# Attention, a dense expert layer and soft mixture on one core: the score exponentials one step later, values and scores in fixed PSUM banks

## The chip, the cores and the metric

The kernel runs on one core of one Trainium2 chip. The metric is the device time of one execution in microseconds (us). Engines go by the profile's names: PE does the matmuls (PEld is its weight load), DVE is VectorE, ACT is ScalarE, POOL is GpSimd, SP issues the DMAs. Each engine executes its own instructions in the order in which the kernel wrote them.

## What is computed

Windowed attention with eight memory keys (4 batches, 8 heads, 768 positions, chunks of 32 queries against 56 keys and the 8 memory keys), a dense layer with a SiLU, and a soft mixture of 8 experts with 4 slots each. Cut to what matters:

```python
# attention, per chunk of 32 queries
scores = scale * np.matmul(q_c, k_full.transpose(0, 1, 3, 2))
scores = scores - np.max(scores, axis=-1, keepdims=True)
a = np.exp(scores)
a = a / (np.sum(a, axis=-1, keepdims=True) + 1e-09)
out[:, :, c_start:c_end] = np.matmul(a, v_full)

# dense layer on x = attention output, 3072 tokens x 512
h = x @ w_in                               # 512 -> 2048
g = h * (1.0 / (1.0 + np.exp(-h)))
x = g @ w_out                              # 2048 -> 512

# soft mixture: logits = x @ phi, 32 slots
d = exp(logits - logits.max(0)); d /= d.sum(0)      # dispatch
slot_input = d.T @ x                                # 32 x 512
slot_out[e] = np.maximum(slot_input[e] @ w1[e], 0) @ w2[e]
c = exp(logits - logits.max(1)); c /= c.sum(1)      # combination
return c @ slot_out
```

## The kernel before

**Tiling.** The 3072 tokens are cut into seven blocks (`BLOCKS`, 256, 384, four of 512, and 384 tokens), numbered j = 0 to 6. The attention works on 24 groups g of 128 tokens. A block's dense layer is done in 16 steps i, one for each slice f of 128 hidden units. Blocks 0 and 1 and the attention that feeds them are written out by hand in a table of words (`OPENING`). From about 120 us on, the loop over j = 2 to 6 and i = 0 to 15 is used, and all that follows is about this loop.

**One step of the loop.** In the order of the code: `emit_h` puts 12 matmuls of 512 columns into one of two PSUM banks that alternate (0 and 1; name `ps_h`, line L399); then the first list of the step, `run(j, i, 0)`; then `g_tanh` (ACT, L419, reads `ps_h`), `g_mult` (DVE, L423, reads the same bank and frees it), `g_turn` (DVE transpose, L427); then the second list, `run(j, i, 1)`. Since `ps_h` has two banks, the matmuls of step i + 2 can't start before `g_mult` of step i is done. I write tanh(i), mult(i) and h(i) for the tanh, the multiply and the 12 matmuls of step i.

**What the lists hold.** Two helpers fill them.

`place(j, i, values, scores)` lays out a piece of the attention of the next block, at steps 5, 8, 11 and 14 (in block 2 also at step 1, there without values). In the first list of step i stand the matmuls of the values of one group (`a_values_turned`, name `ps_x`, L352) and of the scores of the group two further on (`a_scores`, name `ps_s`, L266). In the second list of step i stand the copies of the values (`a_hi` on ACT, L186, and `a_lo` on DVE, L382), the row maxima of the scores (`a_max`, DVE, L274, with L278 where a group lies at a sequence's edge), the subtraction of them (`a_sub`, DVE, L287, with a memset L290 at an edge) and the exponential (`a_exp`, ACT, L293, in place). In the second list of step i + 1 stand the sum (`a_sum`, DVE, L297), the reciprocal (`a_inv`, L300 and L301) and the scaling on POOL (`a_norm`, L191).

`routing(j, i, b)` lays out the soft mixture's work on block b: at steps i + 3 and i + 4 the slot sums (`route_slots`, PE, name `ps_a`, L544, in banks 4 to 7) and their addition into `acc` (`route_acc`, DVE, L555, four instructions, one for each bank in the order 4 to 7; all four in one step for block 1), at i + 7 `route_c` (the combination weights' maximum and subtraction on DVE, L563 and L564, and their exponential on ACT, L565), at i + 9 their normalization (`route_cn`, DVE, L571 to L574). i is 0, and 4 for block 1, whose routing runs in block 2 together with that of block 0.

At steps 2, 6, 9, 12 and 15 (from step 15 of block 2 to the end of block 5) the second list also has a conversion of a weight tile (`wo_conv`): two ACT instructions (L206, L208), then one on DVE (L214) that needs both. `v_turn` (DVE, L339 and L343) transposes a group's weights, one step before its values are computed or a little earlier.

**Banks.** A tile asked for with bank `None` gets the next of a ring of four (4, 5, 6, 7 in this loop), by `mbank`. Scores take two from the ring, then values two, and so on. Counted out, every pair of scores in this loop gets banks 5 and 6, and every pair of values 7 and 4.

**The end.** In the last block the loads of the experts' weights start (`load_ew`), each into a buffer as it comes free; behind the loop follow the experts and the combination, on PE, with 64 tiles of 512 KB to load.

Of the kernel before, what the change touches and what calls it, by code (L numbers as in the profile page):

```python
# [17 lines left out]
BLOCKS = [256, 384, 512, 512, 512, 512, 384]  # L18
# [34 lines left out]
def attn_moe_softmoe_kernel(  # L53
# [15 lines left out]
    L = NB - 1  # L69
    win, woutt, wout = (w.bitcast(U32).rearrange("f p (n two) -> f p n two", two=2) for w in (win64, woutt64, wout64))  # L70
    tok0 = [sum(BLOCKS[:j]) for j in range(NB)]
# [42 lines left out]
    call = const.tile([128, NT, 32], F32, name="call")  # L114
# [6 lines left out]
    def bank(b, shape, name):  # L121
        if b is None:
            return mbank(shape, name)
        return psum.tile(shape, F32, tag=f"b{b}", name=name)

    def mbank(shape, name):
        misc[1] += 1
        return bank(misc[0][misc[1] % len(misc[0])], shape, name)
# [125 lines left out]
    xh_t, xl_t, ps_t, a_t, mx_t, sm_t, at_t = {}, {}, {}, {}, {}, {}, {}  # L254
# [62 lines left out]
    def a_values(g, *bs):  # L317
        if g >= FIRST_TURNED:
            return a_values_turned(g)
        AT, vt = at_t.pop(g), v_t.pop(g)  # L320
        px = ps_t[g] = [bank(b, [128, 2, 128], "ps_x") for b in bs or (None, None)]
        for c in range(4):
            q = slice(32 * c, 32 * c + 32)
            for u in range(2):
                for s, r in ((0, 0), (1, 1), (0, 1), (1, 0)):
                    k, h = slice(64 * s, 64 * s + 64), slice(64 * r, 64 * r + 64)
                    n = 2 * r + u
                    nc.tensor.matmul(px[s][h, u, q], vt[k, n, c], AT[k, n, q], start=True, stop=True)  # L328
# [15 lines left out]

    def a_values_turned(g):
        AT, vt = at_t.pop(g), v_t.pop(g).rearrange("p a b c -> p (a b c)").rearrange("p (h a e) -> p h a e", h=8, a=2)
        px = ps_t[g] = [bank(None, [128, 4, 64], "ps_x") for _ in range(2)]
        for a in range(2):
            for p in range(4):
                for s, r in ((0, 0), (1, 1), (0, 1), (1, 0)):  # L350
                    k, h = slice(64 * s, 64 * s + 64), slice(64 * r, 64 * r + 64)
                    nc.tensor.matmul(  # L352
                        px[s][h, 2 * (p % 2) + p // 2, 32 * a:32 * a + 32], vt[k, 4 * r + p, a], AT[k, 4 * r + p, a],
                        start=True, stop=True,
                    )
# [203 lines left out]
    def route_c(j):  # L559
        nt, d0 = BLOCKS[j] // 128, tok0[j] // 128  # L560
        cs = call[:, d0:d0 + nt]
        mx = sm_p.tile([128, nt, 1], F32, tag="cm", name="cm")
        nc.vector.tensor_reduce(out=mx, in_=cs, axis=AX.X, op=ALU.max)  # L563
        nc.vector.tensor_tensor(out=cs, in0=cs, in1=mx.to_broadcast([128, nt, 32]), op=ALU.subtract)  # L564
        nc.scalar.activation(out=cs, in_=cs, func=ACTF.Exp)  # L565

    def route_cn(j):
        nt, d0 = BLOCKS[j] // 128, tok0[j] // 128
        cs = call[:, d0:d0 + nt]
        cm = sm_p.tile([128, nt, 1], F32, tag="cs", name="cs")  # L570
        nc.vector.tensor_reduce(out=cm, in_=cs, axis=AX.X, op=ALU.add)  # L571
        nc.vector.tensor_scalar(out=cm, in0=cm, scalar1=1e-9, scalar2=None, op0=ALU.add)
        nc.vector.reciprocal(out=cm, in_=cm)
        nc.vector.tensor_tensor(out=cs, in0=cs, in1=cm.to_broadcast([128, nt, 32]), op=ALU.mult)  # L574
# [16 lines left out]
    def load_ew(*places):  # L591
        for p in places:
            if not ew_order:
                ew_free.append(p)
                continue
            m = ew_order.pop(0)
            nc.sync.dma_start(out=p, in_=(w1 if m < 32 else w2)[m % 32])
            ew_t[m] = p
# [4 lines left out]
    def words(t, lo, hi):  # L603
        return [t[:, o:o + 1024] for o in range(lo, hi, 1024)]
# [21 lines left out]
    def at(j, i, half, fn, *args, first=False):  # L626
        work = slots.setdefault((j, i, half), [])
        work.insert(0 if first else len(work), (fn, args))


    def place(j, i, values, scores):
        if values is not None:
            at(j, i, 0, a_values, values)
            at(j, i, 0, load_v, values + 1)
            at(j, i, 1, a_hi, values)
            at(j, i, 1, a_lo, values)
        if scores < NG:
            at(j, i, 0, a_scores, scores)
            at(j, i, 0, load_qk, scores + 1)
            at(j, i, 1, a_max, scores)  # L640
            at(j, i, 1, a_sub, scores)
            at(j, i, 1, a_exp, scores)
            at(j, i + 1, 1, a_sum, scores)
            at(j, i + 1, 1, a_inv, scores)
            at(j, i + 1, 1, a_norm, scores, "p")

    def routing(j, i, b):
        at(j, i, 0, route_keep, b)
        at(j, i + 1, 0, route_sum, b)
        at(j, i + 1, 0, route_max, b)  # L650
        at(j, i + 1, 1, route_exp, b)
        at(j, i + 1, 1, route_turn, b)
        at(j, i + 2, 1, route_call, b)
        at(j, i + 3, 0, route_slots, b)
        at(j, i + 3, 1, route_acc, b, range(4) if b == 1 else (0, 1))
        at(j, i + 4, 1, route_run, b)
        if b != 1:
            at(j, i + 4, 1, route_acc, b, (2, 3))
        at(j, i + 7, 1, route_c, b)
        at(j, i + 9, 1, route_cn, b)  # L660

    QUADS = {2: (8, 11, 14), L: (5, 8, 12)}
    ZLAG = {2: 3}
    for b in (0, 1):
        routing(2, 4 * b, b)
    for j in range(3, NB):
        at(j, 0, 0, logits, j - 1, f_order(j - 1)[-1] // 4)
        routing(j, 0, j - 1)

    TURNS = {2: (0, 4, 7, 10, 13)}  # L670
    for n, i in enumerate((1, 5, 8, 11, 14)):
        g = tok0[3] // 128 - 1 + n
        at(2, TURNS[2][n], 1, v_turn, g + 1)
        place(2, i, g if n else None, g + 2)
    for j in range(3, L):
        for n, i in enumerate((5, 8, 11, 14)[:BLOCKS[j + 1] // 128]):
            g = tok0[j + 1] // 128 + n
            if g + 1 < NG:
                at(j, i - 1 if n else 3, 1, v_turn, g + 1, first=(n == 0))
            place(j, i, g, g + 2)  # L680
# [10 lines left out]
    with tc.manual_schedule():  # L691
# [127 lines left out]
        for c in range(4):  # L819
# [5 lines left out]
            )  # L825
        load_ew(*words(z, 5120, NF * BLOCKS[L]))
        route_c(L)
        route_cn(L)

        def expert1(qd, cs, ph):  # L830
# [203 lines left out]
```

## Time and profile before

| | |
|---|---|
| median of three runs | 488.1 us (486.65 to 488.53) |
| the profiled execution, its own time | 487.32 us |
| its span, first to last instruction | 485.5 us |
| PE busy | 451.4 us, 93% |
| PEld busy | 340.0 us, 70% |
| DVE busy | 344.1 us, 71% |
| ACT busy | 185.0 us, 38% |
| POOL busy | 43.8 us, 9% |
| mean granted TensorE clock | 0.966 of full speed |

The profiled execution took 1.8 us more than its span, and stands 0.8 us below the median. A row of a timeline gives the start, the duration, the engine, the line, the operation, and in brackets how long the engine stood idle before it and which instruction ended that. The span of a matmul is modelled: consecutive matmuls of one h(i) overlap in the rows, so that the time from start to start is what one costs. Rows of the same kind are merged (x2, x36); their duration is then that of the whole group.

### The profile page before, as it was taken

To read this page: it belongs to the slowest core of one execution; us is meant where nothing else is said; L and a number is where in the kernel's file an instruction comes from. 1 tells how busy PE (TensorE), PEld (TensorE's weight loads), DVE (VectorE), ACT (ScalarE), POOL (GpSimd) and SP (SyncE) were. 2 spreads that over 40 slices of the span, in tenths; PEclk is the share of its full clock that TensorE was granted. 3 is DMA by queue.
4 is the path that set the end of the run, shared out by engine and by line. 5 is a ranking of instruction groups with operands and counts; after the bars stand their busy time and mean duration, and the time that the engine had idled before them with its cause. 6 is when DMAs were issued, how large, how long until landed. Compare 5 with 4: busy or idle time off the path is not lost.

```text
span 485.5 us, 14527 instructions
## 1 busy us (share of the span) xinstructions
PE 451.4 (93%) x6373; PEld 340.0 (70%) x6373; DVE 344.1 (71%) x770; ACT 185.0 (38%) x388; POOL 43.8 (9%) x41
## 2 busy tenths in 40 slices
PE   5799999999998989999799999899999999999981
PEld 2689888988785667677667678676787789543641
DVE  4827797887898888888888778888875665531161
ACT  3648787873332123233324133351333222211041
POOL 0412134200000001010011011110100000000000
PEclk9659999999999999999999999999999999999996
DMA  8937687554130224124441234311222997799998
GB/s 329 373 139 269 253 300 284 173 200 141 53 96 13 89 93 176 52 96 140 140 139 63 77 134 168 137 69 45 90 88 96 393 408 275 278 412 408 407 355 267
DMA packets 29728, 93.68 MB, mean 193 GB/s; under 512 B 2784, under 2 KB 9184, under 8 KB 29664
## 3 DMA queue, kind: packets, MB, share of 16 engines
q1 hardware_dynamic: 29664, 92.74, 52.0%
q8 instruction: 50, 0.82, 0.7%
q14 instruction: 14, 0.11, 0.1%
HBM read 86.44 MB, written 6.29 MB: 191 GB/s over the span
## 4 chain that ended last, share of the span: by engine, by line
PE 69%; DVE 18%; DMA 5%; ACT 3%; issue 2%; SPq 1%; DVEq 0%; ACTq 0%
PE ps_h L399 41%; PE ps_a L544 5%; PE ps_l L442 4%; DVE garena L423 3%; PE ps_o L868 3%; DVE z L427 3%; PE ps_e L836 3%; PE ps_x L328 3%; DMA oarena<-in_woutt_dram 2%; DMA oarena<-in_win_dram 2%; PE ps_s L266 2%; PE ps_x L352 2%; DVE oarena L343 1%; PE ps_f L918 1%; ACT garena L419 1%
## 5 line engine op out<-in xcount | busy, mean ns | idle before, releaser
L399 PE MATMUL ps_h<-x,w 128*128 128x512 f32 (+2 forms) x704 | 154.3, 364 | 4.5 <-DVE garena L423 3.9
L399 PE MATMUL ps_h<-x1a,w 128*128 128x512 f32 (+2 forms) x544 | 140.7, 364 | 5.1 <-DVE garena L423 3.9
L399 PEld LDWEIGHTS ps_h<-x,w 128*128 128x128 f32 x704 | 126.3, 192 | 25.8 <-DVE garena L423 5.3
L399 PEld LDWEIGHTS ps_h<-x1a,w 128*128 128x128 f32 x544 | 99.6, 189 | 26.8 <-issue 7.7
L423 DVE SCALAR_TENSOR_TENSOR garena<-garena,ps_h 128x512 f32<-128x512 f32 (+2 forms) x112 | 68.0, 607 | 56.6 <-ACT garena L419 55.7
L419 ACT ACTIVATE garena<-ps_h 128x512 f32<-128x512 f32 (+2 forms) x112 | 59.3, 532 | 121.4 <-PE ps_h L399 109.3
L427 DVE STREAM_TRANSPOSE z<-garena 128x512 f32<-128x512 f32 (+2 forms) x112 | 70.1, 631 | 4.0 <-PE ps_a L544 0.4
L191 POOL TENSOR_TENSOR aarena<-aarena,smm 128x512 f32<-128x512 f32 x19 | 22.7, 1194 | 237.2 <-DVE smm L301 213.9
L214 DVE SCALAR_TENSOR_TENSOR oarena<-oarena 128x512 uint32<-128x512 uint32 x46 | 32.5, 720 | 5.3 <-ACT oarena L208 5.2
L206 ACT ACTIVATE oarena<-oarena 128x512 f32<-128x512 f32 x46 | 30.3, 665 | 14.7 <-DMA oarena<-in_win_dram 10.3
L293 ACT ACTIVATE aarena<-aarena 128x512 f32<-128x512 f32 x20 | 12.6, 632 | 50.0 <-DVE aarena L287 27.6
L208 ACT ACTIVATE oarena<-oarena 128x512 uint32<-128x512 uint16 x48 | 31.7, 668 | 0.0
L544 PE MATMUL ps_a<-z,d 32*32 32x512 f32 x768 | 27.0, 598 | 0.6 <-DVE d L515 0.6
L399 PE MATMUL ps_h<-x1b,w 128*128 128x512 f32 x64 | 25.0, 391 | 0.0
L442 PE MATMUL ps_l<-garena,aarena 128*32 128x512 f32 (+2 forms) x216 | 25.0, 543 | 0.0
L274 DVE TENSOR_REDUCE mx<-ps_s 128x4 f32<-128x256 f32 x48 | 17.8, 411 | 5.9 <-PE ps_s L266 5.9
L191 POOL TENSOR_TENSOR w<-oarena,w 128x512 fp32r<-128x512 f32 x12 | 15.7, 1307 | 55.1 <-ACT w L186 55.1
L544 PEld LDWEIGHTS ps_a<-z,d 32*32 32x32 f32 x768 | 12.1, 103 | 11.7 <-issue 7.0
L266 PE MATMUL ps_s<-aarena 64*32 64x64 f32 x1280 | 17.2, 224 | 0.7 <-DMA aarena<-in_qk_dram 0.7
L555 DVE SCALAR_TENSOR_TENSOR acc<-acc,al,ps_a 128x512 f32<-128x512 f32 x20 | 13.9, 742 | 2.5 <-PE ps_a L544 2.4
L266 PEld LDWEIGHTS ps_s<-aarena 64*32 64x32 f32 x1280 | 13.9, 105 | 2.1 <-DMA aarena<-in_qk_dram 0.8
L287 DVE TENSOR_TENSOR aarena<-ps_s,mx 128x256 f32<-128x256 f32 x40 | 14.8, 410 | 0.1
(202 smaller groups left out, 459.1 us busy)
## 6 DMA issues: line engine op xcount, KB each, us to landing
aarena<-in_qk_dram SPq DMA_DIRECT2D x20, 608.0 KB, 5.4
aarena<-in_v_dram SPq DMA_DIRECT2D x20, 512.0 KB, 4.2
w<-in_w_dram SPq DMA_DIRECT2D x20, 512.0 KB, 7.2
oarena<-in_win_dram SPq DMA_DIRECT2D x16, 512.0 KB, 5.4
oarena<-in_woutt_dram SPq DMA_DIRECT2D x16, 512.0 KB, 5.6
oarena<-in_wout_dram SPq DMA_DIRECT2D x16, 512.0 KB, 3.2
z<-in_w_dram SPq DMA_DIRECT2D x10, 512.0 KB, 7.6
oarena<-in_w_dram SPq DMA_DIRECT2D x9, 512.0 KB, 10.2
```

The source lines that it names most:

```text
L191: (nc.gpsimd if eng == "p" else nc.vector).tensor_tensor(**kw)
L206: nc.scalar.activation(out=x, in_=hi_w.bitcast(F32), func=ACTF.Prelu, scale=REBIAS, alpha=-(2.0**32))
L208: nc.scalar.activation(out=lo_w, in_=raw.bitcast(U16)[:, :, 1], func=ACTF.Copy, scale=2.0**-13, bias=-4095.75 / 8192)
L214: nc.vector.scalar_tensor_tensor(out=xb, in0=xb, scalar=3, in1=lo_w, op0=ALU.logical_shift_left, op1=ALU.bitwise_or)
L266: nc.tensor.matmul(ps[r][q, p], t[h, p, q], t[h, p, w:w + 64], start=True, stop=True)
L274: nc.vector.tensor_reduce(out=mx[:, 4 * r:4 * r + 4], in_=ps_t[g][r], axis=AX.X, op=ALU.max)
L399: nc.tensor.matmul(ph, w_t[f][:, wi, 128 * c:128 * c + 128], x[c], start=(c == 0 and m == 0), stop=(c == 3 and m == 2),)
L419: nc.scalar.activation(out=g_tile(j, f), in_=h_t[j, f], func=ACTF.Tanh, scale=0.5)
L423: nc.vector.scalar_tensor_tensor(out=g, in0=g, scalar=1.0, in1=h_t.pop((j, f)), op0=ALU.add, op1=ALU.mult)
L427: nc.vector.transpose(out=z_view(j)[:, slot], in_=g_t[j, f])
L442: nc.tensor.matmul(rt[j, "pl"][32 * m:32 * m + 32], wp[:, f], g_t[j, f], start=(k == ks[0]), stop=(k == ks[-1] or j == L and m > 1 and k = ...
L544: nc.tensor.matmul(ps[q][32 * cg:32 * cg + 32], d[p, t], zv[p, :, t], start=(b < 4), stop=(b >= nb - 4), tile_position=(32 * q, 32 * cg),)
```

## The change

Three edits, all in the lists of the loop. The table `OPENING` and the arithmetic are as they were.

- `a_exp` goes from the second list of step i into that of step i + 1. It keeps its place ahead of `a_sum`.
- The exponential of `route_c` becomes a function of its own, `route_ce`, and goes from the second list of step 7 into that of step 8 (of steps 7 and 11 into those of steps 8 and 12 in block 2). At the end of the kernel, where there are no steps, it is called right behind `route_c`.
- In the loop the scores are given banks 6 and 7, and the values banks 4 and 5, in place of two of the ring.

```diff
     def a_values_turned(g):
...
-        px = ps_t[g] = [bank(None, [128, 4, 64], "ps_x") for _ in range(2)]
+        px = ps_t[g] = [bank(b, [128, 4, 64], "ps_x") for b in (4, 5)]
...
         nc.vector.tensor_reduce(out=mx, in_=cs, axis=AX.X, op=ALU.max)
         nc.vector.tensor_tensor(out=cs, in0=cs, in1=mx.to_broadcast([128, nt, 32]), op=ALU.subtract)
+
+    def route_ce(j):
+        cs = call[:, tok0[j] // 128:(tok0[j] + BLOCKS[j]) // 128]
         nc.scalar.activation(out=cs, in_=cs, func=ACTF.Exp)
...
         if scores < NG:
-            at(j, i, 0, a_scores, scores)
+            at(j, i, 0, a_scores, scores, 6, 7)
             at(j, i, 0, load_qk, scores + 1)
             at(j, i, 1, a_max, scores)
             at(j, i, 1, a_sub, scores)
-            at(j, i, 1, a_exp, scores)
+            at(j, i + 1, 1, a_exp, scores)
             at(j, i + 1, 1, a_sum, scores)
...
         at(j, i + 7, 1, route_c, b)
+        at(j, i + 8, 1, route_ce, b)
         at(j, i + 9, 1, route_cn, b)
...
         route_c(L)
+        route_ce(L)
         route_cn(L)
```

ACT in block 2, from the copies of the values in step 8 on. L186 are these copies, L293 is the exponential of the scores, L419 are the tanhs (a x3 is three steps), and L565 is the exponential of the combination's weights. Before:

```order
L186 ACTIVATE x_71<-ps_x 128x4x64 x2
L293 ACTIVATE aarena<-aarena 128x512
L419 ACTIVATE garena<-ps_h 128x512 x3
L565 ACTIVATE call<-call 128x96
L186 ACTIVATE x_71<-ps_x 128x4x64 x2
L293 ACTIVATE aarena<-aarena 128x512
L419 ACTIVATE garena<-ps_h 128x512 x3
```

The same place in the changed kernel, up to tanh(14):

```order
L186 ACTIVATE x_71<-ps_x 128x4x64 x2
L419 ACTIVATE garena<-ps_h 128x512
L293 ACTIVATE aarena<-aarena 128x512
L419 ACTIVATE garena<-ps_h 128x512 x2
L186 ACTIVATE x_71<-ps_x 128x4x64 x2
L419 ACTIVATE garena<-ps_h 128x512
L568 ACTIVATE call<-call 128x96
L293 ACTIVATE aarena<-aarena 128x512
L419 ACTIVATE garena<-ps_h 128x512 x2
```

Each exponential of scores now has one tanh ahead of it that stood behind it, and the combination's (L565, now L568) stands behind the copies of step 11 and tanh(12) where it stood ahead of the copies.

ACT in block 3, from the copies of step 8 to tanh(11); L206 and L208 are the conversion of step 9. Before:

```order
L186 ACTIVATE x1a<-ps_x 128x4x64 x2
L293 ACTIVATE aarena<-aarena 128x512
L419 ACTIVATE garena<-ps_h 128x512
L206 ACTIVATE oarena<-oarena 128x512
L208 ACTIVATE oarena<-oarena 128x512
L419 ACTIVATE garena<-ps_h 128x512 x2
```

After:

```order
L186 ACTIVATE x1a<-ps_x 128x4x64 x2
L419 ACTIVATE garena<-ps_h 128x512
L293 ACTIVATE aarena<-aarena 128x512
L206 ACTIVATE oarena<-oarena 128x512
L208 ACTIVATE oarena<-oarena 128x512
L419 ACTIVATE garena<-ps_h 128x512 x2
```

The exponential now stands between tanh(9) and the conversion; the order behind it is the old one. The orders on PE, DVE and POOL are the same in both kernels; the DMAs keep theirs on SP.

## Rows read from the trace of the kernel before

**Rows 1.** The page, chain of work that ended last: shares by engine.

```profile
PE 69%; DVE 18%; DMA 5%; ACT 3%; issue 2%; SPq 1%; DVEq 0%; ACTq 0%
```

**Rows 2.** Timeline, PE: start, duration, instruction, idle before. Blocks 2 to 4.

```profile
155.00 1.14 PE L352 MATMUL ps_x<-oarena,aarena 64*64 64x32 f32 x64 [1.65 <-DVE acc L555]
...
162.21 0.39 PE L399 MATMUL ps_h<-x1a,w 128*128 128x512 f32 x1
163.70 0.19 PEld L399 LDWEIGHTS ps_h<-x1a,w 128*128 128x128 f32 x1 [1.53 <-DVE garena L423]
163.70 0.50 PE L399 MATMUL ps_h<-x1a,w 128*128 128x512 f32 x1 [1.10 <-DVE garena L423]
...
176.53 0.50 PE L399 MATMUL ps_h<-x1a,w 128*128 128x512 f32 x1 [1.30 <-DVE garena L423]
...
241.09 4.50 PE L399 MATMUL ps_h<-x,w 128*128 128x512 f32 x12 [2.78 <-DVE garena L423]
...
306.85 1.19 PE L399 MATMUL ps_h<-x1a,w 128*128 128x512 f32 x4 [1.53 <-DVE garena L423]
```

**Rows 3.** Stretches: length, busy time by engine, PEclk, DMA share, GB/s.

```profile
241.00:246.00 5.00, 4.92 (x20) 3.45 (x20) 4.81 (x11) 0.90 (x2) 1.33 (x1) 0.67 0.29 104
246.00:260.00 14.00, 14.00 (x190) 10.44 (x183) 11.61 (x28) 5.67 (x11) 1.33 (x1) 1.00 0.36 121
...
424.00:485.00 61.00, 49.22 (x751) 26.05 (x737) 17.46 (x44) 12.52 (x31) 0.53 (x1) 0.93 0.99 374
```

**Rows 4.** Timeline, DVE and ACT, block 3, end of step 11 to mult(13).

```profile
238.16 0.76 DVE L287 TENSOR_TENSOR aarena<-ps_s,mx 128x256 f32<-128x256 f32 x2
238.99 0.11 DVE L290 MEMSET aarena<- 32x64 f32 x1
239.20 0.63 ACT L293 ACTIVATE aarena<-aarena 128x512 f32<-128x512 f32 x1 [6.73 <-DVE aarena L290]
239.73 0.58 ACT L419 ACTIVATE garena<-ps_h 128x512 f32<-128x512 f32 x1
...
240.34 0.69 DVE L423 SCALAR_TENSOR_TENSOR garena<-garena,ps_h 128x512 f32<-128x512 f32 x1 [1.24 <-ACT garena L419]
240.77 0.66 ACT L208 ACTIVATE oarena<-oarena 128x512 uint32<-128x512 uint16 x1
...
241.32 0.57 ACT L419 ACTIVATE garena<-ps_h 128x512 f32<-128x512 f32 x1
...
242.71 0.65 DVE L214 SCALAR_TENSOR_TENSOR oarena<-oarena 128x512 uint32<-128x512 uint32 x1
...
243.28 0.68 DVE L423 SCALAR_TENSOR_TENSOR garena<-garena,ps_h 128x512 f32<-128x512 f32 x1
```

**Rows 5.** Timeline, block 3: h(9) to h(11), and step 8 into step 9.

```profile
222.23 8.46 PE L399 MATMUL ps_h<-x,w 128*128 128x512 f32 x36
...
224.80 0.74 DVE L287 TENSOR_TENSOR aarena<-ps_s,mx 128x256 f32<-128x256 f32 x2
...
226.79 0.69 DVE L423 SCALAR_TENSOR_TENSOR garena<-garena,ps_h 128x512 f32<-128x512 f32 x1 [1.25 <-ACT garena L419]
...
230.73 0.60 ACT L419 ACTIVATE garena<-ps_h 128x512 f32<-128x512 f32 x1 [2.12 <-PE ps_h L399]
```

**Rows 6.** Timeline, DVE, block 2: mult(6), the additions into acc, mult(9), copies, mult(12).

```profile
146.87 0.69 DVE L423 SCALAR_TENSOR_TENSOR garena<-garena,ps_h 128x512 f32<-128x512 f32 x1 [1.24 <-ACT garena L419]
...
152.24 2.71 DVE L555 SCALAR_TENSOR_TENSOR acc<-acc,al,ps_a 128x512 f32<-128x512 f32 x4
...
162.96 0.69 DVE L423 SCALAR_TENSOR_TENSOR garena<-garena,ps_h 128x512 f32<-128x512 f32 x1 [1.24 <-ACT garena L419]
...
172.47 0.76 DVE L382 TENSOR_TENSOR x<-ps_x,x 128x256 fp32r<-128x256 f32 x2 [0.62 <-ACT x L186]
...
175.79 0.69 DVE L423 SCALAR_TENSOR_TENSOR garena<-garena,ps_h 128x512 f32<-128x512 f32 x1 [1.24 <-ACT garena L419]
```

**Rows 7.** Timeline, DVE, block 4: mult(12).

```profile
306.11 0.69 DVE L423 SCALAR_TENSOR_TENSOR garena<-garena,ps_h 128x512 f32<-128x512 f32 x1 [1.24 <-ACT garena L419]
```

## The prediction, made before the changed kernel ran

> **What bounds the kernel now.** I read the chain that ended last first: 69% of it is PE and 18% DVE, so most of the time PE's own work sets the end, and in some stretches DVE does [rows 1]. PE is busy 93% of the span, which says little, since the rows of its matmuls overlap. What counts is where PE stands still in the loop. The timeline of PE has five such places from 120 us on that are put down to DVE [rows 2]: 1.65 us at 155.00, where the values wait for an addition into `acc`, and 1.10, 1.30, 2.78 and 1.53 us, where 12 matmuls wait for a `g_mult` (L423) that hasn't freed its bank. The reader is to see that they come in three stretches, around 150 to 177, 225 to 241 and 292 to 307 us, and that PE runs on without a gap between these.
>
> Why is that mult late? The end of one such stretch shows it [rows 4]. DVE ends the subtraction of the scores and its memset at 239.10. ACT then does the exponential (239.20), and only behind it tanh(12), at 239.73, although h(12) had been ready for long: ACT stood idle 6.73 us with the exponential at its head, waiting for DVE. mult(12) then waits for that tanh, and DVE is idle for 1.24 us. So DVE waits for ACT, ACT for DVE, in every step that follows a piece of scores. PE waits for both when it has used up its lead of two banks.
>
> [...]
>
> **What PE loses at the five places.** A matmul's row lasts 0.39 us (the one at 162.21, [rows 2]), but within a group they start 0.23 apart (36 in 8.46 us, [rows 5]). So a stop costs 0.16 more than the idle time that the row names: 1.26, 1.46, 2.94 and 1.69. The first (155.00) follows matmuls of another kind, and I take its 1.65 as it stands. Together 9.0 us. To this comes the clock: 12 matmuls took 4.50 us at 241.09 [rows 2], where a third of the 8.46 us of rows 5, with the tail of 0.16 that the last row of a group has, is close to 3.0. That is 1.5 more. So 10.5 us are there to be had, no more, from PE's side.
>
> [...] Here the weight load's row at 163.70 has 1.53 us of idle time, the matmul's 1.10 [rows 2]; from start to start the loss is between them, 1.26. Taken at each stop by the weight loads, the loss would be larger by 0.27 each, some 1.1 us for the four, and the forecast as much lower. I keep the starts.
>
> **The change, part by part.** No instruction is added or taken away, and the time of each stays. The order changes on ACT alone.
>
> *The exponential of the scores.* Behind tanh(i+1) it no longer holds that tanh up, so mult(i+1) follows the subtraction at once, if h(i+1) is ready. What DVE gains is the idle time of 1.24 us. The exponential then runs beside mult(i+1) and `g_turn`, and the sum that needs it comes behind these two.
>
> *Is it covered there?* In the converting steps ACT now has the exponential, the two conversions and tanh(i+2) in a row behind the subtraction. In [rows 4] the row of exponential, tanh(12) and the pair lasts from 239.20 to 241.43, 2.23 us; without tanh(12), which now stands ahead and took some 0.5 (its 0.58 overlap their neighbours), 1.75. DVE wants the pair for L214, which stood 2.37 behind the start of mult(12) (240.34 to 242.71). So 0.6 us of cover is left. tanh(13) began 2.12 behind the exponential, now 1.6, and a mult begins 0.61 behind its tanh (239.73 to 240.34): 2.2 against the 2.94 from mult(12) to mult(13), so 0.7. I put its cost at nothing; if the cover were gone, each such step would pay up to the exponential's 0.53.
>
> *Stretch 1 (block 2).* Four waits of DVE go: 1.24 ahead of mult(6), mult(9) and mult(12), and 0.62 ahead of the copies at 172.47 [rows 6]. The last is there because the copies on ACT stood behind the combination's exponential, which waited for DVE; with `route_ce` a step later they don't. I now go through PE's stops.
> - 155.00: the values wait for banks 7 and 4, and 7 is the last that `acc` frees. The four additions start 1.24 earlier, at 151.0, and take 2.71, so they end at 153.7. The values now need banks 4 and 5, free after two of the four, at 152.4; PE reaches them at 155.00 − 1.65 = 153.35, and the scores, which need 6 and 7, about a microsecond later, at 154.4. No stop is left: 1.65 saved. With the old banks the values would wait until 153.7, so the banks are worth 0.35 of it once the exponential has moved. Alone they would be worth more: the first two additions ended at 153.6 and all four at 154.95, so values and scores would each stop for some 0.3, and 1.1 would be saved.
> - 163.70: mult(9) started at 162.96, now 2.48 earlier, at 160.48, and the matmuls begin 0.74 behind it (162.96 to 163.70), at 161.22. PE would be there at 163.70 − 1.65 − 1.26 = 160.79. So 0.43 of a stop stays, and PE is 2.48 ahead.
> - 176.53: mult(12) started at 175.79, now 4.34 earlier, at 171.45, and its bank is free for them at 172.19. PE gets there at 176.53 − 2.48 − 1.46 = 172.59. No stop: PE is 3.9 ahead.
>
> *Stretch 2 (block 3).* PE comes into it without a stop, as before. At step 9 the subtraction ends at 225.54 (224.80 + 0.74), but tanh(9) also needs h(9), a third of the group of 36: (8.46 − 0.16) / 3 = 2.77 and the 0.16 of its last row, so 225.16. tanh(11) began 0.04 behind the end of the group (230.73 to 222.23 + 8.46), and mult comes 0.61 behind the tanh. That is 225.81 in place of 226.79, 1.0 gained and not 1.25 [rows 5]. At step 12 the memset ends 1.0 earlier, at 238.1; mult(12) follows at once in place of 240.34, 2.2 earlier [rows 4]. PE lost 2.94 there, so it still stops for 0.7. From the four short stops in rows 2 I take it that the clock then stays at its upper level: 1.5 more. Together 3.7.
>
> *Stretch 3 (block 4).* The same pattern, two waits of 1.24, one of them shown [rows 7]: at mult(9) (of which 0.9 by the same working) and at mult(12). DVE gains 2.1, PE lost 1.69 there: all of it comes back, 1.7.
>
> *The rest.* Elsewhere in the loop PE doesn't stop for DVE, so nothing is gained. The end behind the loop goes with it: its loads keep the DMA engines busy at 0.99 from 424 us on [rows 3], but each is issued when a buffer comes free in the last block, so it starts earlier too. The POOL scaling keeps its place behind the sum.
>
> *Sum:* 3.9 + 3.7 + 1.7 = 9.3 us. Against the profiled execution's own 487.3 that gives 478.0. That execution stands 0.8 below the median of the three runs; against the median it would be 478.8. I forecast the middle, **478.4**.
>
> **The bounds.** What the trace doesn't show is an exponential between a tanh and a conversion, and what the clock does behind stops of 0.4 and 0.7 us. Against me: the clock is not regained (+1.5), the cover is gone in the two converting steps that stretches 2 and 3 wait for each (4 × 0.53 = 2.1). For me: the two stops that I left vanish (−1.1), and the run falls where the lowest of before stood (−0.7 against the profiled one). The forecast's own range is 476.2 to 481.0.
>
> **The rivals.**
> - *DVE stays the bound and the waits come back in part.* The 1.24 us go, but the next thing on DVE, the sum, the conversion or `v_turn` behind POOL's scaling, waits instead. For it: DVE has no other pause between the subtraction and mult(13) in rows 4, so every delay there is paid. Against it: the 0.6 us of cover, worked out above. If half of what DVE gains is lost again, PE gets half of the 7.8 us that aren't clock, and the stop in stretch 2 stays over 1.65 us, so that the clock may fall: 487.3 − 3.9 = 483.4, or 482 with the clock.
> - *It doesn't do what it says.* The tanh was late for another reason (its matmuls), and only the banks count: 1.1 us, so 486.2. Against it: the idle 6.73 us of ACT, put down to DVE [rows 4].
> - *Slower: the conversion becomes the late one.* In ten steps (15 of block 2, four each in blocks 3 and 4, 6 of block 5) an exponential now stands ahead of a conversion pair. If ACT's row of exponential, pair and tanh ends later than DVE's own work, L214 waits and mult(i+2) behind it, and PE two steps later. The wait of 1.24 isn't saved then but stands at L214, longer by 0.53: 10 × 0.53 = 5.3, less the banks' 1.1, gives 491.5. It decides once ACT needs 0.6 us more behind the subtraction than rows 4 show. ACT is idle most of the time, so I hold it for unlikely.
>
> **How the numbers follow.** Forecast 0.79; waits that come back in part 0.14; nothing but the banks 0.04; slower 0.03. The range reaches from 476.2 into the first rival: to 482.0. A difference of 0.5%, 2.4 us, is about what a measurement of this kernel can tell from no change. The first two cases lie more than that below 488.1 (under 485.7), the third inside it: faster 0.93, same 0.04, slower 0.03.
>
> **What would show it.** In the profile of the changed kernel the idle time of DVE ahead of L423 with ACT as its end should fall by about 1.2 at each mult behind a piece of scores; the values in step 8 of block 2 should start without idle time; there should be at most two stops of PE on L423 in the loop, each under 1 us, at steps 11 of block 2 and 14 of block 3; the granted clock should stay 1.00 where it was 0.67; and the stretch behind the loop should keep its length. I am wrong if a wait of about 1 us on ACT shows at L297 or L214, if the stop in block 3 stays above 1.6 us, or if the end doesn't move with the loop.

## The result and the profile after

| | before | after |
|---|---|---|
| median, beside each other on one chip | 487.8 us (486.65 to 488.53, 4 runs) | 476.3 us (476.0 to 476.75, 4 runs) |
| ratio, 95% interval | | 0.977 (0.9745 to 0.979) |
| the profiled execution, its own time | 487.32 us | 476.75 us |
| its span | 485.5 us | 474.9 us |

The change makes the kernel 11.5 us faster. The forecast was 478.4, its range 476.2 to 482.0; the time lies at the range's lower end.

The page of the changed kernel: the busy times of the engines, and the shares of the chain that ended last (they answer to [rows 1]).

```profile
PE 450.1 (95%) x6373; PEld 339.6 (72%) x6373; DVE 343.9 (72%) x770; ACT 185.2 (39%) x388; POOL 43.9 (9%) x41
...
PE 81%; DVE 9%; DMA 4%; issue 2%; ACT 1%; SPq 1%; DVEq 0%; ACTq 0%
```

The engines' busy times are those of before within 0.3%. What changed is who waits: DVE's share of the chain is halved, 18% to 9%, and ACT's falls from 3% to 1%. So the end hangs on PE's own work in more of the span.

The waits added up by line and by what ended them: total us, how many, the longest. First before:

```profile
ACT garena L419 <- PE ps_h L399: 109.3, 62, 6.7
...
DVE garena L423 <- ACT garena L419: 55.7, 49, 3.1
...
ACT aarena L293 <- DVE aarena L287: 27.6, 9, 5.4
ACT aarena L293 <- DVE aarena L290: 22.3, 6, 6.7
...
PE ps_h L399 <- DVE garena L423: 7.8, 6, 2.8
```

The changed kernel:

```profile
ACT garena L419 <- PE ps_h L399: 151.8, 78, 6.8
...
DVE garena L423 <- ACT garena L419: 42.9, 41, 2.3
...
ACT aarena L293 <- DVE aarena L290: 7.8, 5, 2.2
...
DVE oarena L214 <- ACT oarena L208: 5.9, 6, 1.6
```

Before, ACT stood 50 us with an exponential at its head, waiting for DVE's subtraction. Now this is 9.5 us by the page, 7.8 of it behind the memset as shown, and ACT's waiting is behind a tanh that waits for its own matmuls, where nothing else could be done. DVE's wait ahead of `g_mult` falls by 12.8 us. PE's wait for `g_mult` falls from 7.8 us to 1.9 in three pieces, of which one (0.8) lies in the opening. The other two are all that PE's timeline still shows in the loop (start, duration, instruction, idle before; it answers to [rows 2]):

```profile
161.69 0.50 PE L399 MATMUL ps_h<-x1a,w 128*128 128x512 f32 x1 [0.32 <-DVE garena L423]
...
235.11 3.03 PE L399 MATMUL ps_h<-x,w 128*128 128x512 f32 x12 [0.78 <-DVE garena L423]
```

The twelve matmuls behind the second stop take 3.03 us where they took 4.50. The clock's windows (length, busy time of PE, PEld, DVE, ACT and POOL, PEclk, DMA share, GB/s) answer to [rows 3]:

```profile
235.00:240.00 5.00, 4.89 (x84) 3.27 (x84) 4.82 (x11) 2.26 (x5) 1.33 (x1) 1.00 0.30 104
...
413.50:474.90 61.40, 49.09 (x751) 26.03 (x737) 17.43 (x44) 12.52 (x31) 0.53 (x1) 0.93 0.98 369
```

In place of 0.67 (241 to 246 us) the granted clock is 1.00 right behind the stop (235 to 240 us). The end behind the loop is as long as before, 66.5 us from the combination's first matmuls (419.0 and 408.4) to the end of the span, and as full of DMAs.

How DVE and ACT now pass the place of [rows 4], block 3, subtraction to mult(13), DVE's rows and then ACT's:

```profile
234.23 0.11 DVE L290 MEMSET aarena<- 32x64 f32 x1
234.37 0.69 DVE L423 SCALAR_TENSOR_TENSOR garena<-garena,ps_h 128x512 f32<-128x512 f32 x1
...
235.73 0.64 DVE L297 TENSOR_REDUCE smm<-aarena 128x8 f32<-128x512 f32 x1
...
236.73 0.65 DVE L214 SCALAR_TENSOR_TENSOR oarena<-oarena 128x512 uint32<-128x512 uint32 x1
237.30 0.68 DVE L423 SCALAR_TENSOR_TENSOR garena<-garena,ps_h 128x512 f32<-128x512 f32 x1
```

```profile
234.43 0.63 ACT L293 ACTIVATE aarena<-aarena 128x512 f32<-128x512 f32 x1 [2.19 <-DVE aarena L290]
234.97 0.65 ACT L206 ACTIVATE oarena<-oarena 128x512 f32<-128x512 f32 x1
235.53 0.66 ACT L208 ACTIVATE oarena<-oarena 128x512 uint32<-128x512 uint16 x1
236.09 0.57 ACT L419 ACTIVATE garena<-ps_h 128x512 f32<-128x512 f32 x1
```

mult(12) starts 0.03 behind the memset's end, not 1.24. The exponential runs beside it and beside `g_turn`, and ends at 235.06, well ahead of the sum at 235.73. The conversion pair ends at 236.19 (235.53 + 0.66), and DVE wants it at 236.73: 0.54 us of cover is left.

### The profile page after: what moved, and what is told of

It is laid out like the page before. It is cut to its first block, busy times and chain, and to the rows that moved or that the text cites. A ratio compares the mean times of both kernels' runs of the same rounds, so it can differ in the third digit from the quotient of the medians.

```text
span 474.9 us, 14537 instructions
## 1 busy us (share of the span) xinstructions
PE 450.1 (95%) x6373; PEld 339.6 (72%) x6373; DVE 343.9 (72%) x770; ACT 185.2 (39%) x388; POOL 43.9 (9%) x41
## 4 chain that ended last, share of the span: by engine, by line
PE 81%; DVE 9%; DMA 4%; issue 2%; ACT 1%; SPq 1%; DVEq 0%; ACTq 0%
PE ps_h L399 50%; PE ps_a L544 5%; PE ps_l L442 4%; PE ps_s L266 3%; PE ps_o L873 3%; PE ps_e L841 3%; PE ps_x L328 3%; PE ps_x L352 3%; DMA oarena<-in_woutt_dram 3%; DMA acc<-in_qk_dram 2%; DVE garena L423 2%; PE ps_t L311 1%; PE ps_f L923 1%; DVE z L427 1%; PE ps_q L235 1%
## 5 line engine op out<-in xcount | busy, mean ns | idle before, releaser
L419 ACT ACTIVATE garena<-ps_h 128x512 f32<-128x512 f32 (+2 forms) x112 | 59.8, 534 | 166.5 <-PE ps_h L399 151.8
L206 ACT ACTIVATE oarena<-oarena 128x512 f32<-128x512 f32 x46 | 30.4, 665 | 17.3 <-DMA oarena<-in_win_dram 12.4
L214 DVE SCALAR_TENSOR_TENSOR oarena<-oarena 128x512 uint32<-128x512 uint32 x46 | 32.5, 720 | 6.1 <-ACT oarena L208 5.9
L208 ACT ACTIVATE oarena<-oarena 128x512 uint32<-128x512 uint16 x48 | 31.6, 667 | 0.0
L293 ACT ACTIVATE aarena<-aarena 128x512 f32<-128x512 f32 x20 | 12.6, 628 | 9.5 <-DVE aarena L290 7.8
```

What stands on the lines that cost most here:

```text
L206: nc.scalar.activation(out=x, in_=hi_w.bitcast(F32), func=ACTF.Prelu, scale=REBIAS, alpha=-(2.0**32))
L208: nc.scalar.activation(out=lo_w, in_=raw.bitcast(U16)[:, :, 1], func=ACTF.Copy, scale=2.0**-13, bias=-4095.75 / 8192)
L214: nc.vector.scalar_tensor_tensor(out=xb, in0=xb, scalar=3, in1=lo_w, op0=ALU.logical_shift_left, op1=ALU.bitwise_or)
L419: nc.scalar.activation(out=g_tile(j, f), in_=h_t[j, f], func=ACTF.Tanh, scale=0.5)
```

## Where PE's time came from, place by place

The best ruler is PE itself, since its order is the same in both kernels. The values of each piece (L352) stand at steps 5, 8, 11 and 14 of a block. Some of these rows of the changed kernel, in blocks 2 to 4:

```profile
139.02 1.14 PE L352 MATMUL ps_x<-aarena 64*64 64x32 f32 x64
153.80 1.14 PE L352 MATMUL ps_x<-oarena,aarena 64*64 64x32 f32 x64
...
176.85 1.14 PE L352 MATMUL ps_x<-oarena,aarena 64*64 64x32 f32 x64
...
239.07 1.13 PE L352 MATMUL ps_x<-oarena,aarena 64*64 64x32 f32 x64
267.50 1.14 PE L352 MATMUL ps_x<-aarena 64*64 64x32 f32 x64
278.71 1.14 PE L352 MATMUL ps_x<-oarena,aarena 64*64 64x32 f32 x64
...
300.20 1.14 PE L352 MATMUL ps_x<-oarena,aarena 64*64 64x32 f32 x64
```

Beside them the starts of the same instructions before. The profiled execution of the changed kernel came out of the opening 0.57 us later (139.02 against 138.45, ahead of all that the change touches); that is taken out in the fourth column, and in every comparison of two traces below.

| values of | before | after | gained, opening taken out | in this stretch | predicted |
|---|---|---|---|---|---|
| block 2, step 5 | 138.45 | 139.02 | 0 | | |
| block 2, step 8 | 155.00 | 153.80 | 1.77 | 1.77 | 1.65 |
| block 2, step 11 | 167.64 | 165.63 | 2.58 | 0.81 | 0.83 |
| block 2, step 14 | 180.47 | 176.85 | 4.19 | 1.61 | 1.46 |
| block 3, step 5 | 209.15 | 205.28 | 4.44 | 0.25 | 0 |
| block 3, step 11 | 230.62 | 226.72 | 4.47 | 0.03 | 0 |
| block 3, step 14 | 246.51 | 239.07 | 8.01 | 3.54 | 3.7 |
| block 4, step 5 | 274.95 | 267.50 | 8.02 | 0.01 | 0 |
| block 4, step 8 | 287.45 | 278.71 | 9.31 | **1.29** | 0 |
| block 4, step 11 | 297.69 | 288.94 | 9.32 | 0.01 | 0 |
| block 4, step 14 | 310.79 | 300.20 | 11.16 | 1.84 | 1.7 |

Behind this the gain stays: the combination's first matmuls stand at 419.0 before and 408.4 after, 10.6 or, with the 0.57, 11.2. The three predicted stretches give 9.6 of it for 9.3 predicted. One piece of 1.29 us had no term in the prediction. Before, PE's timeline in step 6 of block 4 reads:

```profile
276.81 0.50 PE L399 MATMUL ps_h<-x1a,w 128*128 128x512 f32 x1
278.42 0.85 PE L399 MATMUL ps_h<-x1a,w 128*128 128x512 f32 x3 [1.12 <-issue]
```

Between the first and the second matmul of h(6) PE stands 1.12 us, put down to "issue", that is to nothing that the profile shows. In the changed kernel this stop is absent.

## The experiments

Two theories stood at the outset. **A:** the gain comes from the order on ACT; the exponential at ACT's head held up a tanh, and so DVE and PE; the cover of some 0.6 us at L214 decides whether this goes on being free. **B:** a rival in each run: the banks carry the gain, or only single steps count. The diffs are against the kernel named. The kernel before ran beside them on the same chips, at medians of 488.3 to 488.6.

### Only the banks (e1, against before)

```diff
-        px = ps_t[g] = [bank(None, [128, 4, 64], "ps_x") for _ in range(2)]
+        px = ps_t[g] = [bank(b, [128, 4, 64], "ps_x") for b in (4, 5)]
...
-            at(j, i, 0, a_scores, scores)
+            at(j, i, 0, a_scores, scores, 6, 7)
```

> The kernel before with the fixed banks alone: values in 4 and 5, scores in 6 and 7, both exponentials where they were. Theory A (the prediction's rival: the banks save the stop at the values of step 8 in block 2 for themselves): 1.1 us faster, ratio 0.998. Theory B (DVE sets the stretch): the stop at the values shrinks from 1.65 us to some 0.3, PE reaches the 12 matmuls of step 11 about 1.1 us earlier and waits there for the same mult(9), so that stop grows from 1.10 to some 2.2 us, and the time is that of before, 487.8 (ratio 1.000). Should that longer stop take the clock to its lower level, the time is above before by up to 1.5.

Measured: 486.8 us, ratio 0.996 (0.995 to 0.9975). PE's stops in the loop:

```profile
154.67 1.13 PE L352 MATMUL ps_x<-oarena,aarena 64*64 64x32 f32 x62 [0.16 <-DVE acc L555]
164.68 0.50 PE L399 MATMUL ps_h<-x1a,w 128*128 128x512 f32 x1 [2.18 <-DVE garena L423]
177.50 0.50 PE L399 MATMUL ps_h<-x1a,w 128*128 128x512 f32 x1 [1.27 <-DVE garena L423]
242.01 4.57 PE L399 MATMUL ps_h<-x,w 128*128 128x512 f32 x12 [2.82 <-DVE garena L423]
306.53 1.20 PE L399 MATMUL ps_h<-x1a,w 128*128 128x512 f32 x4 [1.53 <-DVE garena L423]
```

The banks do cut the stop at the values, from 1.65 us to 0.16, and by step 11 all of it is given back: the stop there grows from 1.10 to 2.18, since mult(9) on DVE is as late as before. So the 1.1 us that the prediction gave the banks alone is wrong. What e1 does gain is at another place: the "issue" stop of block 4 is absent, and PE is 1.28 us earlier behind it, while the medians lie 1.8 us apart; the rest is not accounted for.

### All but the banks (e2, against after)

The reverse of e1's diff, on the changed kernel.

> The changed kernel with the ring of banks as before: both exponentials a step later, values in 7 and 4, scores in 5 and 6. Theory A: it lacks what the banks save, 0.35 us at the values of step 8 in block 2 and no more: 476.7. Theory B (DVE sets the stretch): a stop of some 0.3 us at these values takes the place of the 0.32 at step 11, and the time is that of the change, 476.3, ratio to before 0.977. If the banks carried the gain, 480 or more.

Measured: 478.4 us (475.2 to 479.6), ratio 0.9765 (0.972 to 0.981). PE's stops:

```profile
155.93 1.14 PE L352 MATMUL ps_x<-oarena,aarena 64*64 64x32 f32 x64 [0.52 <-DVE acc L555]
236.72 3.02 PE L399 MATMUL ps_h<-x,w 128*128 128x512 f32 x12 [0.78 <-DVE garena L423]
272.38 0.84 PE L399 MATMUL ps_h<-x1a,w 128*128 128x512 f32 x3 [0.90 <-issue]
```

The stop at the values is the larger one here, 0.52, but none is left at step 11, and block 2 ends with a gain of 4.16 against 4.19. So in blocks 2 and 3 the exponentials' place is worth all, the banks nothing. What e2 lacks against the changed kernel is again the "issue" stop, which costs it 1.1: 10.0 gained in the loop for 11.2. The two medians can't be told apart.

### One exponential at a time (e3 against after, e4 against before)

e3 moves the scores' exponential only, with the banks. e4 moves the combination's only, without the banks.

```diff
-        at(j, i + 8, 1, route_ce, b)
+        at(j, i + 7, 1, route_ce, b)
```

> The changed kernel, but the exponential of the combination's weights stays in its old step (7, and 7 and 11 in block 2). Theory: the 0.62 us of DVE ahead of the copies of step 11 in block 2 come back, mult(12) is that much later, of which PE has some 0.4 to spare; the stop returns with 0.2 to 0.3 and the time is 476.6. If the two exponentials counted alike (one step's wait each), a quarter of the gain, 2.8 us, would go: 479.

> The kernel before with only the exponential of the combination's weights a step later, the scores' exponential and the ring of banks as before. Theory: 0.62 us of DVE ahead of the copies of step 11 in block 2 go, so the stop at step 14 of block 2 falls from 1.30 to 0.7; nothing else moves: 487.2, ratio 0.999, not to be told from before. The other stops (1.10, 2.78, 1.53) and the clock of 0.67 behind the 2.78 stay. For the stop of 1.12 us in step 6 of block 4 that no engine explains (at 278.42 in the trace of before, absent in that of the change): if it belongs to this order of the program it is here at the same matmul; if it is chance it may be elsewhere or missing.

Measured: e3 477.15 us, ratio 0.976 (0.974 to 0.978); e4 487.2 us, 0.997 (0.994 to 0.999). In e3's trace some 0.25 us are lost against the changed kernel, all of it by step 14 of block 2 (3.91 gained for 4.19). In e4's the stop there falls to 0.60 us, and 0.68 are gained in block 2; the stops of blocks 3 and 4 stay:

```profile
155.65 1.51 PE L352 MATMUL ps_x<-oarena,aarena 64*64 64x32 f32 x64 [1.70 <-DVE acc L555]
...
176.46 0.50 PE L399 MATMUL ps_h<-x1a,w 128*128 128x512 f32 x1 [0.60 <-DVE garena L423]
241.02 4.61 PE L399 MATMUL ps_h<-x,w 128*128 128x512 f32 x12 [2.82 <-DVE garena L423]
278.30 0.85 PE L399 MATMUL ps_h<-x1a,w 128*128 128x512 f32 x3 [0.90 <-issue]
```

At step 11 of block 2 the expectation fails: the stop of 1.10 us is not there. PE was late by itself. Behind the stop at the values (1.70 us, the first row) the 64 matmuls took 1.51 us in place of 1.14; what made them slower is not shown. PE so reached the 12 matmuls of step 11 only when mult(9) had freed their bank, and nothing was lost by it.

So with fixed banks the scores' exponential carries 9.3 of the 9.6. The combination's is worth 0.7 alone and 0.3 on top of the other.

### Using up the cover (e5 and e6, against after)

In the converting steps L206, which writes one tile from another, is done three times (e5) or five times (e6). The output is the same; the additional time is ACT's alone, ahead of L208, and so of L214 on DVE.

```diff
-        for k in range(4):
+        for k in [0] * 2 + [0, 1, 2, 3] if WO[u][1] != 2 else range(4):
```

(e6 has `[0] * 4`.)

> The changed kernel with the first instruction of the weight conversion (L206, 0.65 us, a start every 0.56) done three times over in place of once, in the steps 6, 9, 12 and 15 that convert, right behind the exponential of the scores: 1.12 us more of ACT in each, with the same output. This is a test of the cover. Theory A (the prediction's: 0.6 us of cover in every such step): L214 is 0.5 us late in each, and the stop in block 3 grows by up to 1.0, so 477 to 478. Theory B (the cover that counts is that of step 9, where the combination's normalization gives DVE 0.8 us more to do ahead of L214, 1.7 in the trace of the change, since mult(12) decides): nothing, 476.3.

> As the one before with four extra conversions' first instructions, 2.24 us more of ACT in each of those steps. Theory A: L214 is 1.6 us late in each, the stops of blocks 3 and 4 grow by 2 to 3 us each, and the clock falls in block 3: 482 or more. Theory B: L214 and mult(10) in step 9 are some 0.55 late, the stop in block 3 goes from 0.78 to some 1.3, block 4 loses 0.2, the clock stays 1.00: 477.1.

Measured: e5 481.75 us, ratio 0.9855 (0.9825 to 0.9885), 4.3 us slower in the loop than the changed kernel; e6 491.8 us, 1.0075 (1.005 to 1.010), slower than before. DVE's waits at L214 and one of its rows in e5, at the place shown above:

```profile
DVE oarena L214 <- ACT oarena L208: 13.7, 16, 1.7
```

```profile
239.57 0.95 DVE L214 SCALAR_TENSOR_TENSOR oarena<-oarena 128x512 uint32<-128x512 uint32 x1 [0.79 <-ACT oarena L208]
```

The same place on ACT in e5:

```profile
236.94 2.04 ACT L206 ACTIVATE oarena<-oarena 128x512 f32<-128x512 f32 x3
238.88 0.65 ACT L208 ACTIVATE oarena<-oarena 128x512 uint32<-128x512 uint16 x1
```

And in e6 the waits at L214:

```profile
DVE oarena L214 <- ACT oarena L208: 27.7, 17, 2.5
```

L206 to L208 is now 1.94 us (236.94 to 238.88), where it was 0.56: the two repeats add 1.38. DVE waits 0.79 of this, so 0.59 was covered, beside the 0.54 read from the changed kernel's own rows. With the repeats the waits at L214 go from 5.9 us (all of it in the opening) to 13.7 and 27.7, and the time from 476.3 to 481.75 and 491.8. This is the rival "the conversion becomes the late one", brought about by the repeats: it exists, at this place it starts where the prediction put it (some 0.6 us), and in the change as it is the exponential stays under it. The times expected for e5 were too low, because a repeat costs 0.70 and not 0.56, and because the loss isn't confined to the stop of block 3: from step 5 of block 3 to step 5 of block 5 the values stand 127.51 us apart in e5 (206.43 to 333.94) and 123.33 in the changed kernel (205.28 to 328.61). That is 4.2 us of the 4.3. They are lost in both blocks, and mostly from step 11 on: 0.7 and 1.4 between steps 11 and 14 of blocks 3 and 4, 1.15 and 0.7 between step 14 and step 5 of the next block, and only 0.3 in all between steps 5 and 11. L214 itself waits 0.6 to 1.05 us in steps 6, 12 and 15 of both blocks, but in step 9 not at all (block 3) or for 0.25 (block 4). So theory B was right that step 9 has more cover than the others, and wrong that step 9 decides.

### The two stops that are left (e9, against after)

The `g_turn` of step 8 in block 2 and of step 11 in block 3 is deferred until behind the next `g_mult`, which so starts 0.7 us earlier.

```diff
-                if i >= ZLAG.get(j, 0):
+                if i >= ZLAG.get(j, 0) and (j, i) not in ((2, 8), (3, 11)):
```

> The changed kernel with one transpose into z (L427, 0.71 us) of DVE moved behind the next multiply, at the two places where PE still stops: the one of step 8 of block 2 goes behind mult(9), that of step 11 of block 3 behind mult(12). Theory: both mults come some 0.7 us earlier, so the stop of 0.32 us at step 11 of block 2 goes and that of 0.78 at step 14 of block 3 falls to about 0.1; together 1.1 us, 475.2, of which the comparison can just see the half. If the waits move to something behind these mults (the two transposes in a row ahead of the sum and the conversion), the stops shrink and others come up: 476.3.

Measured: 475.2 us (474.55 to 477.6), ratio to before 0.9745 (0.972 to 0.977). No stop of PE is left in the loop, and the trace has 0.54 us more gained in block 2 and 0.73 in block 3, 1.27 together. By the trace this version is ahead of the changed kernel; the times' intervals overlap, so they alone don't settle it.

### The "issue" stop (e7, e8, e10, e11, e12)

In e1 it went with the banks, in e2 it came back with the ring. The profile names no wait there. One other thing differs: counted on PE, with the waits that stand as instructions of their own, the first matmul of that step has place 2527 with the ring and 2534 with fixed banks, since these need seven more waits ahead of it (the expectation of e7 counted eight). Theory A: the place decides. Theory B: the ring's banks do. The number of warm-up matmuls at the program's start shifts the place by two each.

```diff
-        keep_warm(10)
+        keep_warm(18)
```

(e7: the ring, 18. e12: the ring, 11. e8, e10 and e11: fixed banks, 2, 6 and 7.)

> The changed kernel with the ring of banks as before (as e2_no_banks) and eight more warm-up matmuls at the very start of PE (18 in place of 10), so that all that follows on PE stands eight instructions further on in its stream. By the fixed banks PE's stream has nine instructions more (semaphore waits), eight of them ahead of step 6 of block 4. Theory A (the stop of some 1 us in that step belongs to a place in the stream of instructions): it is gone or elsewhere. Theory B (it belongs to the banks, 7 and 4 against 4 and 5): it is there, 0.9 to 1.1 us, at the second matmul of the step. The time of the run says nothing here, since the start of the kernel differs.

> The changed kernel, fixed banks and all, with eight warm-up matmuls fewer at the very start of PE (2 in place of 10), so that PE's stream stands at step 6 of block 4 about where it stands with the ring. Theory A (a place in the stream): the stop of some 1 us comes back at that step. Theory B (the banks): no stop there. The time says nothing here, since the start differs.

> The changed kernel with 6 warm-up matmuls in place of 10 at the very start. Counted in the built program, the first matmul of step 6 of block 4 then stands at place 2526 of PE's stream (an instruction of the source counted as one; each warm-up matmul is two). With the stop of about 1 us it stood at 2527 (ring of banks, three kernels), without it at 2534 (fixed banks), 2518 (fixed banks, e8) and 2543 (ring, e7). Theory A (a place in the stream, whatever the banks): the stop of 0.9 to 1.1 us is here, at the second or third matmul of the step. Theory B (the ring's banks, with something else that e7 changed): none.

> As the one before with 7 warm-up matmuls: place 2528. Theory A: the stop of 0.9 to 1.1 us is here, or in the one before, or in both, and in this one an instruction or so earlier in the step. Theory B: none.

> The changed kernel with the ring of banks and 11 warm-up matmuls: place 2529. Theory A: as at 2528, so the same as in the kernel with fixed banks there. Theory B (the ring): the stop of 0.9 to 1.1 us is here and not in the two with fixed banks. If it is in none of the three, only 2527 itself shows it so far, and the cause stays open.

| kernel | banks | place | time, us | "issue" stop |
|---|---|---|---|---|
| before, e2, e4 | ring | 2527 | 488.1, 478.4, 487.2 | 1.12, 0.90, 0.90 |
| e12 | ring | 2529 | 476.5 | 1.79 |
| e7 | ring | 2543 | 476.8 | none |
| e8 | fixed | 2518 | 476.6 | none |
| e10, e11 | fixed | 2526, 2528 | 476.5, 476.9 | none |
| after, e1, e3, e5, e6, e9 | fixed | 2534 | as above | none |

e7, e8 and e10 to e12 are one run each. e12's stop, at the start of the same step:

```profile
269.17 1.09 PE L399 MATMUL ps_h<-x1a,w 128*128 128x512 f32 x4 [1.79 <-issue]
```

It costs e12 1.8 us (12.98 from the values of step 5 to those of step 8, for 11.21 in the changed kernel); that its time is no longer than the others' comes from an opening some 2 us shorter in that run. e7 speaks against the ring as the only cause, e10 and e11, which put fixed banks at the places on both sides of the ring's, against the place as the only one. Seen in four of five kernels with the ring and in none of nine with fixed banks, the stop goes with the ring, and e7 is left over. What PE waits for there, and what the ring has to do with it, **stays open**.

## Why the prediction was right, and where it was off

*What bounds the kernel.* Right: the chain of tanh, exponential and mult was the cause, and with the two exponentials moved all three stretches come back with no other edit (e2).

*Stretch 1, 3.9 predicted, 4.19 measured.* The four waits of DVE that answer to [rows 6] are gone, by its rows in the changed kernel:

```profile
146.23 0.69 DVE L423 SCALAR_TENSOR_TENSOR garena<-garena,ps_h 128x512 f32<-128x512 f32 x1
...
161.02 0.62 DVE L423 SCALAR_TENSOR_TENSOR garena<-garena,ps_h 128x512 f32<-128x512 f32 x1
...
169.74 0.75 DVE L382 TENSOR_TENSOR x<-ps_x,x 128x256 fp32r<-128x256 f32 x2
...
171.73 0.67 DVE L423 SCALAR_TENSOR_TENSOR garena<-garena,ps_h 128x512 f32<-128x512 f32 x1
```

The remaining stop was put at 0.43 from start to start. Its idle time is 0.32; with the 0.16 by which a row of a matmul outlasts the distance of two starts, that is 0.48. The sum also lacked a term: the matmul behind a stop is followed by the next after 0.34 us (163.70 to 164.04 before) and not after 0.23, so a stop that goes gives 0.11 more than the prediction's price.

*Stretch 2, 3.7 predicted, 3.54 measured.* The stop of 0.7 came as 0.78 idle (0.94 by starts), and the clock's 1.5 was regained (3.03 us for the twelve matmuls in place of 4.50, with a granted clock of 1.00). That the clock stays up behind a short stop was the author's estimate from four stops of up to 1.65 us; it held here, and no run shows up to what length of a stop it holds. The step ahead of the stop was right in kind: mult(9) still waits for a tanh that waits for its matmuls, as the row that answers to [rows 5] shows, 0.38 in place of 1.25, so 0.87 gained for 1.0.

```profile
222.02 0.69 DVE L423 SCALAR_TENSOR_TENSOR garena<-garena,ps_h 128x512 f32<-128x512 f32 x1 [0.38 <-ACT garena L419]
```

*Stretch 3, 1.7 predicted, 1.84 measured.* Right, with no stop left.

The three stretches are 9.57 for 9.3. The prediction's other price for a stop, by the weight loads' idle time, is 0.27 higher. It would not have moved the sum by 1.1 us: at the stops of 163.70 and 241.09 what PE gains is set by `g_mult`, whatever the stop cost, so only the two others count, 0.54. At these two the starts gave 1.46 and 1.69, the weight loads 1.73 and 1.96, and the trace 1.61 and 1.84. It lies between, and the 0.11 above is most of what the starts lacked.

*The cover.* Right: 0.54 left for 0.6, nothing waits at L214 in blocks 2 to 4 at that place, and e5 and e6 show what lies beyond.

*The banks.* Wrong, though without weight in the sum. The step that failed is "alone they would be worth more … and 1.1 would be saved": it followed the saving to the scores of the same step and not to the next `g_mult`, which was the later of the two (e1). And with the exponential moved, the 0.35 given to the banks is not seen at the end of block 2 (4.16 without them, 4.19 with them).

*The missing term.* "Elsewhere in the loop PE doesn't stop for DVE, so nothing is gained" holds but for 0.25 us, and the search for stops took only those put down to DVE. The stop of 1.12 us on "issue" was in the same timeline, and its going gave 1.29 of the 11.2. It is the main part of the 2.1 us between forecast and median. Of the rest, 0.3 is the three stretches, 0.25 a gain between step 14 of block 2 and step 5 of block 3, and 0.4 the choice of a forecast above the sum; that the changed kernel's profiled execution lies 0.45 above its median is about made up for by the 0.57 of its opening. The 0.25 is mostly a stop for DVE inside a group of matmuls, where no row names it. In the first of these rows, from before, the eight matmuls read `garena`, to which `g_mult` still wrote until 188.18; in the second, from the changed kernel, it was done at 183.06:

```profile
187.99 1.29 PE L442 MATMUL ps_l<-garena,aarena 128*32 128x512 f32 x8
...
184.35 1.06 PE L442 MATMUL ps_l<-garena,aarena 128*32 128x512 f32 x8
```

This `g_mult` too had waited 1.24 us for a tanh behind an exponential before, and waits 0.20 now.

*The rivals.* "DVE stays the bound" didn't come: no wait of DVE in block 3 took the place of the one removed. "Only the banks" is refuted by e2, which has none of them and gains 10.0 in the loop. "Slower" needs what e6 adds.

## What to carry to other kernels

On an engine that works in order, look for the instruction at its head that waits for engine X while X waits for something behind it: here the exchange of two neighbours on ACT, with no work saved, gave 2%. Before moving it, measure the cover at the place it moves to, from the end of what it delays to the start of who needs that (0.54 us here), because past it the gain shrinks (e5, with 1.4 us more ahead of L214), and with 2.8 us more the same change is a loss (e6). A stop that an edit removes is only worth what the next late partner allows (e1: 1.5 us saved and given back 10 us later), so follow a gain to the end of its block before it is added up.

## What the runs showed of the hardware

- *The clock.* Before, behind a stop of PE of 2.78 us at step 14 of block 3, the granted clock was 0.50 from 241 to 244 us (0.67 from 241 to 246) and 1.00 from 246 on. Behind stops of 2.82 us at the same place it was 0.72 in e1 (241 to 247) and 0.66 in e4 (241 to 246). It was 1.00 behind the 1.65 us at the values of step 8 in block 2 before (155 to 160), behind the 2.18 us in block 2 of e1 (162 to 170) and behind the 1.59 us in block 3 of e6 (239 to 245). Behind the 1.70 us in block 2 of e4 the 64 matmuls of the values took 1.51 us in place of 1.14; what the clock was there is not shown. What decides when it falls is not shown either. The windows of e1 at its two stops (PEclk is the third number from the end):

```profile
162.00:170.00 8.00, 5.82 (x120) 3.70 (x119) 6.39 (x17) 2.20 (x4) 1.04 (x1) 1.00 0.01 2
...
241.00:247.00 6.00, 4.99 (x20) 3.51 (x20) 5.55 (x11) 1.81 (x4) 1.33 (x1) 0.72 0.26 86
```

  The price in block 3 was some 1.5 us each time: 12 matmuls took 4.50 to 4.61 us (before, e1, e4) where they take 3.03 in the changed kernel.
- *Stops on "issue".* In the loop PE stood 0.9 to 1.8 us on "issue" (1.12 before, 0.90 in e2 and e4, 1.79 in e12), in step 6 of block 4 of every kernel that showed it, and edits with no work in that step (banks in e1, eight more warm-up matmuls at the start in e7) made it vanish. What PE waited for is not shown. e2 and the changed kernel differ by 1.1 us in the loop for this alone.
- *Repeats on ACT.* L206 three times in a row took 2.04 us (e5), 0.70 from start to start; from L206 to L208 it is 0.56 (234.97 to 235.53 in the changed kernel).
